# Spectral weights in rows of 4096 B: one transfer a tile for rows 256 to 511

## The chip, the cores and the metric

The kernel runs on one core of a Trainium2 chip. The time is device microseconds of one execution; of each kernel several executions are taken, and the median counts.

## What is computed

Forgetting attention over 8 batches and 8 heads (576 positions, 64 wide), then a spectral mix over the 512 joined channels, and a channel mix with a residual:

```python
attn = softmax(scale * q @ k.T + decay)          # causal, decay from cumsum(log f)
x = (attn @ v) joined over heads                 # [8, 576, 512]
X = np.fft.rfft(x, axis=1)                       # 64 modes are kept
Yr = einsum('bmd,mde->bme', Xr, w_r) - einsum('bmd,mde->bme', Xi, w_i)
Yi = einsum('bmd,mde->bme', Xr, w_i) + einsum('bmd,mde->bme', Xi, w_r)
u = x + np.fft.irfft(Y, n=576, axis=1)
out = u + np.maximum(u @ w_ch, 0.0)
```

`w_r` and `w_i` are [64, 512, 512] in f32, 67 MB each. The kernel works in bf16 with f32 sums; the transfers that GpSimd (POOL) issues convert on the way.

## The kernel before

**Attention.** 32 pairs (four groups `g` of two heads, 8 batches `b`, in the order of `g`). In each step `i` of a loop, POOL issues the loads of pair `i+3` (`load_qk` line 107, `load_v` line 119), VectorE (DVE) scales v (line 319), TensorE (PE) makes the scores (line 351) and the weighted sums (line 396), ScalarE (ACT) the exponentials (line 358), and q and k of the next pair are transposed (line 306; copied by DVE, line 311). Two steps later `dft` (line 423) turns the finished 128 channels of one group and batch into a spectrum: five matmuls over the 576 positions with a table of three blocks of 64 modes (-im, re, im), summed in one PSUM tile of 128 channels x 192. ACT copies it (line 430) into `XS[channel, g, ...]`, where one mode's 24 columns (three blocks x 8 batches) lie together.

**Weights.** Modes are taken in 16 units `u` of four, channels in four quarters `dc` of 128 rows of each matrix. A tile (u, dc) holds a quarter of four modes of both matrices, as bf16 [128, 2, 4, 512]: two transfers (`w_r`, `w_i`), each 4 x 128 rows of 2048 B at the source, 1024 B in SBUF. The list `wseq` has all (u, 0), then (0, 1) to (5, 1), then the rest by unit. Tiles have 7 buffers; in program order POOL is 6 tiles ahead of the matmuls. A transfer of POOL's queue also waits for the one eight transfers before it, whose completion semaphore it takes over.

**Spectral matmuls.** `spec_mms` (line 160) has eight matmuls for a tile, four modes in four strips of 32 PSUM partitions: the 32 (16 and the neighbours') spectrum columns as weights, 512 columns of `w8` moving. From step 10 on `spec_early` takes one tile of the list's first 22 in each attention step. The last unit runs the other way around: `spec_cols` (line 175) has the `w8` blocks as weights and 16 spectrum columns moving, 32 matmuls for a tile.

**After attention**, for each unit: the remaining quarters (2 and 3, from unit 6 on also 1); for eight of them `xw` (lines 535 and 549), which multiplies x with `w_ch`; from unit 12 on `fold` (lines 591 to 597), which adds the first 96 of 128 real and imaginary parts of the spectrum back for a batch; then the sums `Yb` (line 631) are turned by matmuls with `perm` (line 634). In the last unit, quarter 3 is split: 16 matmuls of `w_r`, an add, the first output block's bases (line 672), 16 matmuls of `w_i`, an add (line 730). Then 20 blocks of output (`rest`, line 687, ACT line 745, DVE line 746) leave on SyncE's queue.

The order is written out by hand (a manual schedule); nothing is moved by a planner.

Of the kernel before, what the change touches and what calls it, by code (L numbers as in the profile page):

```python
# [10 lines left out]
F32 = mybir.dt.float32  # L11
BF16 = mybir.dt.bfloat16
I32 = mybir.dt.int32
ALU = mybir.AluOpType
# [9 lines left out]
def kernel(  # L24
# [11 lines left out]
    nc = tc.nc  # L36
    B, H, S, Dh = q.shape
    NM = moe_w_r.shape[0]
    D = H * Dh
    assert S == 576 and Dh == 64 and D == 512 and H == 8, (B, H, S, Dh)  # L40
    assert NM == 64 and B == 8
    NSB = 5
    SBLK = [128, 128, 128, 128, 64]
    NEB = D // 128
    BH = B * H
    NPAIR = B * H // 2
    NU = NM // 4
# [5 lines left out]
    XROW = 24 * NM + 32  # L53
# [8 lines left out]
    const = ctx.enter_context(tc.tile_pool(name="const", bufs=1))  # L62
    wpool = ctx.enter_context(tc.tile_pool(name="wpool", bufs=NW))
    yxpool = ctx.enter_context(tc.tile_pool(name="yxpool", bufs=8))

    x_all = const.tile([128, B, NSB, D], BF16, name="x_all")
    XS = const.tile([128, NEB, XROW], BF16, name="XS")
    wch = const.tile([128, NEB, D], BF16, name="wch")
    ident_bf = const.tile([128, 128], BF16, name="ident_bf")
    ident_f = const.tile([128, 128], F32, name="ident_f")  # L70
# [4 lines left out]
    bas3 = const.tile([128, NSB, 3, NM], BF16, name="bas3")  # L75
# [5 lines left out]
    accT = const.tile([128, NEB, B, 8], F32, name="accT")  # L81
# [13 lines left out]
    psM = actx.enter_context(tc.tile_pool(name="psM", bufs=2, space=PSUM))  # L95
# [36 lines left out]


    early = [(u, 0) for u in range(NU)] + [(u, 1) for u in range(NX)]
    wseq = early + [(u, dc) for u in range(NU) for dc in range(1, NEB) if (u, dc) not in early]
    wtile = {}
    wissued = [0]

    def issue_w():
        if wissued[0] >= len(wseq):  # L140
            return
        u, dc = wseq[wissued[0]]
        wissued[0] += 1
        w8 = wpool.tile([128, 2, 4, D], BF16, tag="w8", name="w8")
        for t, src in enumerate((moe_w_r, moe_w_i)):
            step = 1 if t == 1 and wissued[0] == len(wseq) else 4
            for j in range(0, 4, step):
                m = 4 * u + j
                nc.gpsimd.dma_start(  # L149
                    w8[:, t, j : j + step, :],  # L150
                    src[m : m + step, dc * 128 : (dc + 1) * 128, :].rearrange("m p e -> p m e"),
                )
        wtile[(u, dc)] = w8

    def spec_mms(A, u, dc, first, last):
        w8 = wtile.pop((u, dc))
        for t in range(2):
            for j in range(4):
                c0 = (4 * u + j) * 24 + (8 if t == 0 else 0)
                nc.tensor.matmul(  # L160
                    A[32 * j : 32 * j + 32, :],
                    lhsT=XS[:, dc, c0 : c0 + 32],
                    rhs=w8[:, t, j, :],
                    start=(first and t == 0),
                    stop=(last and t == 1),
                )

    def spec_cols(AT, dc, ts):
        u = NU - 1
        w8 = wtile[(u, dc)]  # L170
        for j in range(4):
            for eb in range(NEB):
                for t in ts:
                    c0 = (4 * u + j) * 24 + (8 if t == 0 else 0)
                    nc.tensor.matmul(
                        AT[:, eb, 2 * j : 2 * j + 2, :].rearrange("p c b -> p (c b)"),
                        lhsT=w8[:, t, j, eb * 128 : (eb + 1) * 128],
                        rhs=XS[:, dc, c0 : c0 + 16],
                        start=(t == ts[0]),
                        stop=(t == ts[-1]),  # L180
                    )


# [13 lines left out]
    load_v(0)  # L197
    masks.make_identity(nc, ident_bf[:])
    issue_w()
    load_qk(1)  # L200
    load_v(1)
# [64 lines left out]
    def setup_late():  # L266
        nc.vector.memset(XS[:, :, 24 * NM : XROW], 0.0)
        nc.vector.tensor_copy(
# [148 lines left out]

    def dft(i):
        g, b = pairs[i]
        pd = psM.tile([128, 3, NM], F32, tag="m", name="pd")  # L420
        for sc in range(NSB):
            ns = SBLK[sc]
            nc.tensor.matmul(  # L423
                pd[:],
                lhsT=x_all[:ns, b, sc, g * 128 : g * 128 + 128],
                rhs=bas3[:ns, sc, :, :],
                start=(sc == 0),
                stop=(sc == NSB - 1),
            )
        nc.scalar.copy(  # L430
            XS[:, g, 0 : 24 * NM].rearrange("p (m c b) -> p c m b", c=3, b=8)[:, :, :, b], pd[:]
        )

    yacc = {}
# [1 line left out]
    def spec_early(u, dc):  # L436
        if u == NU - 1:
            AT = psM.tile([128, NEB, 8, B], F32, tag="m", name="AT0")
            spec_cols(AT, dc, (0, 1))
            nc.vector.tensor_copy(accT[:], AT[:].rearrange("p e c b -> p e b c"))  # L440
            return
        A = psM.tile([128, D], F32, tag="m", name="A0")
        spec_mms(A, u, dc, True, True)
        if dc == 0:
            if u % 2 == 0:
                yacc[u // 2] = yxpool.tile([128, 2, D], F32, tag="yx", name="yacc")
            nc.scalar.copy(yacc[u // 2][:, u % 2, :], A[:])
        else:
            y = yacc[u // 2][:, u % 2, :]
            nc.vector.tensor_tensor(y, A[:], y, ALU.add)  # L450
# [9 lines left out]
    for i in range(NPAIR + 2):  # L460
# [35 lines left out]
        if i >= 2:  # L496
            dft(i - 2)
# [8 lines left out]
        if i >= 10 and spec_done < len(early):  # L506
            spec_early(*early[spec_done])
            spec_done += 1
# [3 lines left out]
    with ExitStack() as bctx:  # L512
# [8 lines left out]
        with ExitStack() as mctx:  # L521
# [81 lines left out]
            for u in range(NU):  # L603
                last = u == NU - 1
                if not last:
                    A = psA.tile([128, D], F32, tag="a", name="A1")
                first = 2 if u < NX else 1
                for dc in range(first, NEB - 1 if last else NEB):
                    if dc == NEB - 1 and u in xw_plan:
                        xw(xw_plan[u])  # L610
                    split = NSB
                    if u >= NF and dc < 3:
                        b = 2 * (u - NF) + dc - 1
                        split = 2 if b == B - 1 else NSB
                        ys = fold_modes(b)
                        fold(b, ys, range(split))
                    if last:
                        AT = psA.tile([128, NEB, 8, B], F32, tag="a", name="AT1")
                        spec_cols(AT, dc, (0, 1))
                        nc.vector.tensor_tensor(  # L620
                            accT[:], AT[:].rearrange("p e c b -> p e b c"), accT[:], ALU.add
                        )
                    else:
                        spec_mms(A, u, dc, dc == first, dc == NEB - 1)
                    issue_w()
                    if split < NSB:
                        fold(b, ys, range(split, NSB))
                if last:
                    break
                Yb = ybpool.tile([128, D], BF16, tag="yb", name="Yb")  # L630
                nc.vector.tensor_tensor(Yb[:], A[:], yacc[u // 2][:, u % 2, :], ALU.add)  # L631
                yps = psT.tile([128, NEB, 64], F32, tag="t", name="yps")
                for eb in range(NEB):
                    nc.tensor.matmul(
                        yps[:, eb, :],
                        lhsT=Yb[:, eb * 128 : (eb + 1) * 128],
                        rhs=perm[:],
                        start=True,
                        stop=True,
                    )  # L640
                if u < NF:
                    ydst = YT[:, :, :, 8 * u : 8 * u + 8]
                else:
                    ydst = YL[:, :, :, 8 * (u - NF) : 8 * (u - NF) + 8]
                nc.vector.tensor_copy(
                    ydst,
                    yps[:].rearrange("p eb (b c) -> p eb b c", b=8),
                )

        usb = bctx.enter_context(tc.tile_pool(name="usb", bufs=4))  # L650
        psU = bctx.enter_context(tc.tile_pool(name="psU", bufs=4, space=PSUM))
# [43 lines left out]
        def last_modes(h):  # L695
# [22 lines left out]
            nc.scalar.copy(yl[h][0][:], py[:])  # L718
            nc.vector.tensor_copy(yl[h][1][:], pyw[:])

        AT = psU.tile([128, 2, NEB, 8, B], F32, tag="u", name="AT2")
        spec_cols(AT[:, 0, :, :, :], NEB - 1, (0,))
        nc.vector.tensor_tensor(
            accT[:], AT[:, 0, :, :, :].rearrange("p e c b -> p e b c"), accT[:], ALU.add
        )
        first = bases(0)
        spec_cols(AT[:, 1, :, :, :], NEB - 1, (1,))
        for h in range(2):
            bs = slice(4 * h, 4 * h + 4)
            nc.vector.tensor_tensor(  # L730
                YL[:, :, bs, KL - 8 : KL],
                AT[:, 1, :, :, bs].rearrange("p e c b -> p e b c"),
                accT[:, :, bs, :],
                ALU.add,
            )
# [51 lines left out]
```

## Time and profile before

| what | value |
|---|---|
| median of 3 runs | 457.81 us (457.38 to 460.25) |
| profiled execution | 458.9 us, its span 457.1 us |
| granted TensorE clock | 0.825 |
| busy PE, DVE, ACT, POOL | 75%, 54%, 48%, 42% |
| moved by DMA | 96.66 MB, mean 211 GB/s |
| read from HBM | 163.73 MB |
| first tile with the second half's pace | from 233 us |

A busy PE is not PE at its peak, and an engine's share over the whole span mixes two stages: attention with early tiles up to some 230 us, then the weight stage, then output from 424 us. "DMA share" is the time that packets took over that of 16 DMA engines; packets of one engine overlap, so it can be over 1. GB/s counts what is written, so a converting load reads twice as much.

### The profile page before, as it was taken

The numbers are of one execution on the slowest core, as the hardware profiler recorded it, in microseconds if no ns is written. First come the engines' busy times: TensorE is split into PE (matmuls) and PEld (weight loads), VectorE is DVE, ScalarE is ACT, GpSimd is POOL, SyncE is SP. The second block draws the span as 40 slices with busy tenths as digits, with TensorE's granted clock in tenths as the row PEclk, the third lists the DMA queues.
The fourth block names the chain that finished last, engine by engine and source line by source line (L and its number), as shares of the span: only waits on it lengthen the run. The fifth ranks groups of instructions, "written<-read, shape, count | busy, mean of one in ns | idle before, by whom it ended". The sixth has DMA issues, their size and how long they took to land.

```text
span 457.1 us, 8638 instructions
## 1 busy us (share of the span) xinstructions
PE 343.5 (75%) x3448; PEld 171.7 (38%) x3448; DVE 244.6 (54%) x632; ACT 220.2 (48%) x325; POOL 193.7 (42%) x280
## 2 busy tenths in 40 slices
PE   1587796997787877868988487678666499778993
PEld 1254464554444434543533133223232133234331
DVE  7597786985665747576832122212121066356785
ACT  5476475786656565645722121122022066354673
POOL 9574646957466666565332332233223222310000
PEclk9999677997968787766997767777577599899998
DMA  9999999999999999999999999999999999998598
GB/s 161 204 198 209 197 224 206 170 225 212 222 214 222 217 224 216 224 210 218 208 207 205 206 206 206 206 206 206 207 206 207 207 206 206 206 206 148 197 339 294
DMA packets 89432, 96.66 MB, mean 211 GB/s; under 512 B 8400, under 2 KB 82640, under 8 KB 89392
## 3 DMA queue, kind: packets, MB, share of 16 engines
q0 software_dynamic: 80608, 85.61, 108.7%
q1 hardware_dynamic: 8784, 10.50, 6.9%
q8 instruction: 27, 0.44, 0.4%
q14 instruction: 13, 0.11, 0.1%
HBM read 163.73 MB, written 9.44 MB: 379 GB/s over the span
## 4 chain that ended last, share of the span: by engine, by line
DMA 72%; PE 13%; POOL 6%; DVE 5%; issue 3%; DVEq 0%; POOLq 0%
DMA w<-in_moe_w_i_dram 56%; DMA vt<-in_v_dram 11%; POOL vt L119 3%; DMA qk<-in_k_dram 2%; DMA wch<-in_moe_w_ch_dram 2%; PE U L672 2%; PE Z L672 2%; POOL w L149 2%; DVE qkT L311 2%; PE pav L396 2%; POOL qk L107 1%; PE U L687 1%; PE sps L351 1%; PE pd L423 1%; DVE vs L319 1%
## 5 line engine op out<-in xcount | busy, mean ns | idle before, releaser
L358 ACT ACTIVATE et<-sps 128x1024 bf16<-128x1024 f32 x96 | 96.0, 1042 | 20.7 <-PE sps L351 20.5
L149 POOL DMA_DIRECT2D w<-in_moe_w_r_dram x64 | 48.2, 754 | 84.1 <-DMA w<-in_moe_w_r_dram 24.0
L149 POOL DMA_DIRECT2D w<-in_moe_w_i_dram x67 | 49.8, 744 | 68.6 <-DMA w<-in_moe_w_i_dram 63.1
L160 PE MATMUL A<-w,XS 128*32 128x512 bf16 x480 | 45.7, 448 | 34.5 <-DMA w<-in_moe_w_i_dram 23.4
L556 ACT CAST XW<-pxw 128x512 bf16<-128x512 f32 (+1 forms) x40 | 23.4, 585 | 96.9 <-PE pxw L549 89.5
L396 PE MATMUL pav<-vs,et 128*128 128x65 bf16 (+1 forms) x896 | 58.9, 211 | 0.0
L396 PEld LDWEIGHTS <-et 128*128 128x128 bf16 (+1 forms) x896 | 42.4, 111 | 29.6 <-issue 27.7
L119 POOL DMA_DIRECT2D vt<-in_v_dram x58 | 45.2, 785 | 18.5 <-DMA w<-in_moe_w_i_dram 5.8
L311 DVE COPY qkT<-tp 128x640 bf16<-128x640 bf16 x64 | 48.9, 764 | 6.1 <-PE tp L306 5.9
L351 PE MATMUL sps<-qkT 64*128 64x512 bf16 (+4 forms) x320 | 46.3, 357 | 4.3 <-ACT et L358 2.5
L430 ACT CAST XS<-pd 128x192 bf16<-128x192 f32 x32 | 33.2, 1045 | 32.7 <-PE pd L423 32.6
L631 DVE TENSOR_TENSOR Yb<-A,yacc 128x512 bf16<-128x512 f32 x15 | 10.4, 691 | 69.4 <-PE A L160 69.4
L319 DVE TENSOR_TENSOR vs<-vt,wT 128x512 bf16<-128x512 f32 x32 | 22.1, 689 | 47.4 <-DMA vt<-in_v_dram 47.3
L549 PE MATMUL pxw<-wch,xT 128*128 128x512 bf16 (+1 forms) x160 | 47.0, 457 | 0.0
L306 PE MATMUL tp<-ident_bf,qk 128*64 128x128 bf16 x576 | 32.6, 248 | 13.1 <-DMA qk<-in_k_dram 12.4
L411 DVE TENSOR_TENSOR x_all<-pav,rcp 128x384 bf16<-128x384 f32 (+2 forms) x96 | 36.2, 377 | 3.4
L598 DVE TENSOR_TENSOR XW<-pz,XW 128x512 bf16<-128x512 f32 (+1 forms) x40 | 27.0, 690 | 20.2 <-PE pz L597 19.9
L540 DVE COPY xT<-ptr 128x576 bf16<-128x576 bf16 x32 | 14.6, 457 | 37.8 <-PE ptr L535 37.6
L107 POOL DMA_DIRECT2D qk<-in_k_dram x32 | 19.8, 619 | 31.5 <-DMA w<-in_moe_w_i_dram 29.4
L160 PEld LDWEIGHTS <-XS 128*32 128x32 bf16 x480 | 9.8, 97 | 53.0 <-issue 47.5
L342 PE MATMUL s<-qkT 64*64 64x64 bf16 x64 | 7.3, 213 | 27.9 <-DVE qkT L311 27.9
L306 PEld LDWEIGHTS <-qk 128*64 128x64 bf16 x576 | 21.3, 123 | 18.5 <-DMA qk<-in_q_dram 12.0
(111 smaller groups left out, 510.6 us busy)
## 6 DMA issues: line engine op xcount, KB each, us to landing
w<-in_moe_w_r_dram POOLq DMA_DIRECT2D x64, 512.0 KB, 19.3
w<-in_moe_w_i_dram POOLq DMA_DIRECT2D x63, 512.0 KB, 20.0
out_dram<-o_sb SPq DMA_DIRECT2D x16, 512.0 KB, 3.5
vt<-in_v_dram POOLq DMA_DIRECT2D x58, 128.0 KB, 7.5
qk<-in_q_dram POOLq DMA_DIRECT2D x32, 144.0 KB, 9.4
qk<-in_k_dram POOLq DMA_DIRECT2D x32, 144.0 KB, 8.3
out_dram<-o_sb SPq DMA_DIRECT2D x8, 128.0 KB, 3.3
vl<-in_v_dram POOLq DMA_DIRECT2D x14, 64.0 KB, 7.5
```

Of the source, the lines that this page charges most:

```text
L119: q_v.dma_start(vt[:, 4 * hp : 4 * hp + 4, :], v[b, 2 * g + hp, 0:512, :].rearrange("(c p) d -> p c d", p=128),)
L149: nc.gpsimd.dma_start(w8[:, t, j : j + step, :], src[m : m + step, dc * 128 : (dc + 1) * 128, :].rearrange("m p e -> p m e"),)
L160: nc.tensor.matmul(A[32 * j : 32 * j + 32, :], lhsT=XS[:, dc, c0 : c0 + 32], rhs=w8[:, t, j, :], start=(first and t == 0), stop=(last and ...
L306: nc.tensor.transpose(tp[64 * hp : 64 * hp + 64, r - r0, :, :].rearrange("p n c -> p (n c)"), qk[:, hp, r * 64 : r * 64 + 64], ident_bf[:, :],
L311: nc.vector.tensor_copy(st[i]["T"][:].rearrange("p n (c r) -> p n c r", r=9)[:, :, :, r0:r1], tp[:, 0 : r1 - r0, :, :].rearrange("p r n c ...
L351: nc.tensor.matmul(ps[:, hp, c : c + n], lhsT=KT[sl, jb * 128 : jb * 128 + 128], rhs=QT[sl, i0 : i0 + n], start=True, stop=True,)
L358: nc.scalar.activation(st[i]["et"][:, T, :, :], ps[:], ACT.Exp, scale=scale)
L396: nc.tensor.matmul(pav[:Ms, sb % 3, hp, :], lhsT=eblk(i, hp, jb, sb), rhs=rhs, start=(jb == 0), stop=(jb == sb),)
L411: nc.vector.tensor_tensor(x_all[:ns, b, lo:hi, g * 128 : g * 128 + 128].rearrange("p s (h d) -> p s h d", h=2), pav[:ns, lo % 3 : lo % 3 + ...
L430: nc.scalar.copy(XS[:, g, 0 : 24 * NM].rearrange("p (m c b) -> p c m b", c=3, b=8)[:, :, :, b], pd[:])
L549: nc.tensor.matmul(pxw[:Ms, :], lhsT=xT[:, eb, sb * 128 : sb * 128 + Ms], rhs=wch[:, eb, :], start=(eb == 0), stop=(eb == NEB - 1),)
L598: nc.vector.tensor_tensor(XW[b][:Ms, sb, :], pz[:Ms, :], XW[b][:Ms, sb, :], ALU.add)
```

## The change

Quarters 0 and 1 stay. Rows 256 to 511 of a matrix (quarters 2 and 3) are now taken together: tile (u, 2) is these rows of `w_r` for four modes, tile (u, 3) the same of `w_i`. Partition p takes rows 256 + 2p and 257 + 2p, which lie side by side, 4096 B at the source and 2048 B in SBUF. A tile is one transfer, the last one four (one for each mode; before, the last tile had one transfer of `w_r` and four of `w_i`). The list has the same order of (u, dc).

The spectrum has to be split the same way: even and odd channels of the upper 256. For groups 2 and 3, `dft` runs twice, on channels with a step of two, into 64 PSUM partitions (0 to 63 for group 2, 64 to 127 for group 3), and ACT's copy goes to a new tile `XP[p, even/odd, 24 columns, mode]`, where one column's 64 modes lie together and the 24 columns of a mode are 128 B apart. `XS` keeps groups 0 and 1. In the last unit, quarter 3 is no longer split: its 32 matmuls come after the first bases.

```diff
-    XS = const.tile([128, NEB, XROW], BF16, name="XS")
+    XS = const.tile([128, 2, XROW], BF16, name="XS")
+    XP = const.tile([128, 2, 24, NM], BF16, name="XP")
...
         u, dc = wseq[wissued[0]]
         wissued[0] += 1
-        w8 = wpool.tile([128, 2, 4, D], BF16, tag="w8", name="w8")
-        for t, src in enumerate((moe_w_r, moe_w_i)):
-            step = 1 if t == 1 and wissued[0] == len(wseq) else 4
+        if dc < 2:
+            w8 = wpool.tile([128, 2, 4, D], BF16, tag="w8", name="w8")
+            for t, src in enumerate((moe_w_r, moe_w_i)):
+                nc.gpsimd.dma_start(
+                    w8[:, t, :, :],
+                    src[4 * u : 4 * u + 4, dc * 128 : (dc + 1) * 128, :].rearrange("m p e -> p m e"),
+                )
+        else:
+            w8 = wpool.tile([128, 4, 2, D], BF16, tag="w8", name="w8")
+            src = (moe_w_r, moe_w_i)[dc - 2]
+            step = 1 if wissued[0] == len(wseq) else 4
             for j in range(0, 4, step):
                 m = 4 * u + j
                 nc.gpsimd.dma_start(
-                    w8[:, t, j : j + step, :],
-                    src[m : m + step, dc * 128 : (dc + 1) * 128, :].rearrange("m p e -> p m e"),
+                    w8[:, j : j + step, :, :].rearrange("p m r e -> p m (r e)"),
+                    src[m : m + step, 256:512, :].rearrange("m (p r) e -> p m (r e)", r=2),
                 )
...
+    XPv = XP[:].rearrange("p r c m -> p (r c) m")
...
-        for t in range(2):
+        for n in range(2):
             for j in range(4):
-                c0 = (4 * u + j) * 24 + (8 if t == 0 else 0)
+                m = 4 * u + j
+                st_, sp_ = first and n == 0, last and n == 1
+                if dc < 2:
+                    M = 32
+                    c0 = m * 24 + (8 if n == 0 else 0)
+                    lhsT, rhs = XS[:, dc, c0 : c0 + 32], w8[:, n, j, :]
+                else:
+                    M = 32 if st_ else 16
+                    c0 = 24 * n + (8 if dc == 2 else 0)
+                    lhsT, rhs = XPv[:, c0 : c0 + M, m], w8[:, j, n, :]
                 nc.tensor.matmul(
...
+                    A[32 * j : 32 * j + M, :], lhsT=lhsT, rhs=rhs, start=st_, stop=sp_
+                )
...
+        pd = psM.tile([128, 2, 3, NM], F32, tag="m", name="pd2")
+        half = slice(64 * (g - 2), 64 * (g - 2) + 64)
+        for r in range(2):
+            for sc in range(NSB):
+                ns = SBLK[sc]
+                nc.tensor.matmul(
+                    pd[half, r, :, :],
+                    lhsT=x_all[:ns, b, sc, g * 128 + r : g * 128 + 128 : 2],
+                    rhs=bas3[:ns, sc, :, :],
+                    start=(sc == 0),
+                    stop=(sc == NSB - 1),
+                )
         nc.scalar.copy(
-            XS[:, g, 0 : 24 * NM].rearrange("p (m c b) -> p c m b", c=3, b=8)[:, :, :, b], pd[:]
+            XP[half, :, :, :].rearrange("p r (c b) m -> p r c b m", c=3)[:, :, :, b, :], pd[half]
         )
...
-        AT = psU.tile([128, 2, NEB, 8, B], F32, tag="u", name="AT2")
-        spec_cols(AT[:, 0, :, :, :], NEB - 1, (0,))
-        nc.vector.tensor_tensor(
-            accT[:], AT[:, 0, :, :, :].rearrange("p e c b -> p e b c"), accT[:], ALU.add
-        )
         first = bases(0)
-        spec_cols(AT[:, 1, :, :, :], NEB - 1, (1,))
+        AT = psU.tile([128, NEB, 8, B], F32, tag="u", name="AT2")
+        spec_cols(AT, NEB - 1)
```

`spec_cols` picks its operands for quarters 2 and 3 in the same way as `spec_mms` (16 columns of `XPv` moving, `w8[:, j, n, ...]` as weights).

## The prediction

> **What bounds the kernel now.** I read the page's row of DMA first: the engines are busy in every slice up to the last weights. The table of stretches shows what that means in the second half (columns: stretch, its length, busy time of PE, PE's weight loads, DVE, ACT, POOL with counts, granted clock, DMA share, GB/s).
>
> ```profile
> 120.00:160.00 40.00, 31.48 (x392) 17.80 (x390) 25.47 (x80) 24.36 (x32) 24.72 (x36) 0.74 1.22 218
> ...
> 274.00:314.00 40.00, 28.63 (x180) 12.38 (x181) 8.47 (x18) 5.85 (x10) 11.61 (x16) 0.71 1.24 206
> 314.00:355.00 41.00, 29.00 (x181) 11.73 (x180) 7.01 (x14) 8.77 (x15) 11.85 (x16) 0.75 1.24 206
> ...
> 420.00:424.00 4.00, 3.61 (x50) 1.83 (x48) 1.83 (x5) 1.17 (x2) 0.00 (x0) 1.00 0.10 18
> ```
>
> From 233 to 417 us the rate is 206 GB/s in every stretch, whatever the engines do. The chain of waits says the same as a period:
>
> ```profile
> 253.43 20.05 DMA w<-in_moe_w_i_dram
> 273.77 20.05 DMA w<-in_moe_w_i_dram
> 294.11 20.05 DMA w<-in_moe_w_i_dram
> ```
>
> Eight transfers of 512 KB, four tiles, take 20.34 us from one start to the next: 5.085 us a tile (4 x 1.0486 MB / 20.34 = 206 GB/s). A tile reads twice what it writes (f32 in, bf16 out): 412 GB/s at the source. It has 1024 rows of 2048 B, 64 for each of the 16 DMA engines, so one row takes 79.5 ns. Third, the list of waits: who waits for whom.
>
> ```profile
> DVE vs L319 <- DMA vt<-in_v_dram: 47.3, 19, 3.3
> ...
> PE A L160 <- DMA w<-in_moe_w_i_dram: 23.4, 12, 2.6
> ...
> PE tp L306 <- DMA qk<-in_k_dram: 12.4, 9, 4.0
> ...
> PE A L160 <- DMA w<-in_moe_w_r_dram: 10.4, 9, 1.9
> ```
>
> In both halves the engines wait for the stream, not the stream for them. Last, the end, where the stream meets TensorE (start, length):
>
> ```profile
> 417.28 0.93 PE L175 MATMUL AT<-XS,w 128*128 128x16 bf16 x31 [0.81 <-DMA w<-in_moe_w_i_dram]
> ...
> 420.34 0.56 PE L175 MATMUL AT<-XS,w 128*128 128x16 bf16 x16
> ...
> 420.76 0.59 PE L672 MATMUL U<-x_all,ident_bf 128*128 128x512 bf16 x2
> ...
> 421.26 0.61 PE L672 MATMUL Z<-XW,ident_bf 128*128 128x512 bf16 x2
> ...
> 421.70 0.66 PE L175 MATMUL AT<-XS,w 128*128 128x16 bf16 x16
> ```
>
> The last wait for weights ends at 417.28 (tile (15,2)); from there PE works without a gap into the output blocks. So the time is the stream up to tile (15,2), plus 40 us of PE work and output.
>
> **The change, part by part. The rows.** Sixteen units have two tiles each with the new rows, 32 in all; each becomes 512 rows of 4096 B, 32 for each DMA engine. The order of tiles, the bytes and the buffers (7) stay. What a 4096 B row costs no row of this trace shows; bytes alone make it 2 x 79.5 = 158.9 ns. A fixed part in each row can be read from the attention stage, where short rows are mixed in. At 219 GB/s (160 to 216 us) one pair with one tile (1.0486 + 0.2949 + 0.2949 MB written) takes 7.48 us. Less 5.085 for the tile, 2.40 us are left for q and k (16 rows of 2304 B for each engine) and v (72 rows of 256 B). With a row costing o + s x bytes, two equations hold: o + 2048 s = 79.5 and 88 o + 55296 s = 2400. They give s = 0.0368 ns/B and o = 4.2 ns. A 4096 B row is then 154.7 ns: 4.2 ns saved, 32 times a tile, 0.134 us, and 31 tiles up to (15,2) give 4.2 us. The mix is the weak place: with 222 GB/s (160 to 180 us) o is 2.5 ns and the saving 2.5 us, with 217 (180 to 216 us) 5.2 ns and 5.2 us; if q and k rows cost no more than 2048 B ones, o is 6.6 ns and it is 6.5 us. Zero holds if the source side is limited by bytes. A loss isn't excluded: if v paid for bytes alone (0.71 us), q and k would be left with 1.69 us, 105 ns a row, 18% more per byte than at 2048 B, and 32 tiles at that are +29 us. I take 4.2: the line by the mean rate, with both row lengths on it, in the middle of what the rates of that stage give.
>
> The Trainium skill (DMA: Bandwidth & Descriptors, "Why small descriptors are slow") puts about 3 cycles of overhead on each packet, with 32 B beats at 850 MHz: an estimate by it is 78.8 ns for 2048 B, near the measured 79.5, and 154.1 for 4096 B, which would save 3.5 us over 31 tiles. The same section holds joining descriptors worth it only up to 256 B, which speaks against the change; by that the saving is about 0. The same page ("iDMA fabric") gives a stream with 4 KiB rows 408.7 GB/s, less than the 412 here; by that the 32 tiles cost 1.5 us more. No run here shows 4096 B rows.
>
> **Fewer transfers.** 32 fewer on POOL's queue, about 0.75 us of issue each; they are hidden, since POOL waits for landings (63.1 and 29.5 us before line 149). Transfers wait for the one eight before them; with three tiles in four transfers, six tiles may be under way instead of four, and the buffers allow no fewer. The stream gets no emptier: 0.
>
> **Half a tile can no longer be used early.** PE took four of eight matmuls on the w_r half before the w_i half came; now it waits for the whole, and behind that wait stand Yb's turning matmuls (line 634) and the next unit. At (14,3) that makes 0.40 us after the landing into 0.61, 0.2 later; the wait of 0.81 at 417.28 covers it. Without that cover it is 0.2 at the end.
>
> **The spectrum.** For 16 pairs dft makes ten matmuls instead of five (same 192 columns), 0.69 to 1.09 us more PE work a pair. PE is idle 8.5 of 40 us from 120 to 160, 1.6 us in a pair's 7.5. Where nothing is awaited a pair takes 3.9 us (pd at 220.07 and 224.01), less than a tile's 5.085. So DMA waits hide it: 0; all of it on the path is 16 x 0.69 to 1.09, 11 to 17 us. ACT's copy goes from 1045 ns (192 elements written at a step) to something between 585 (line 556, 512 in a row) and 2090 (twice the elements); ACT is idle some 3 us a pair, so either is hidden.
>
> **Operands at a step of 128 B.** Weights of 16 or 32 columns now come from XP at a step, in the middle tiles under DMA waits of 2.6 to 6.5 us in each 20: 0. In (15,2) and the last tile the step is in the moving operand of 2 x 32 matmuls, now about 30 ns each. No such read is in the trace. The nearest row is ACT's stepped write, 1045/192 = 5.4 ns an element: 16 columns would take 87 ns, 64 x 57 = +3.6 us. A gain has no source there, the columns being the same. I take 0, since the write is another engine's, and keep 3.6 for the range.
>
> **The end.** Sixteen matmuls go from before the first bases to after them (DVE's add of their half falls away). U moves up, Z still waits until 421.26 (the last XW of line 598), then 32 matmuls (0.93) instead of 16 (0.56): +0.4. The last pieces are twice as large, with eight matmuls behind the last one instead of four; no bytes move from 422 on (0 GB/s), and PE would come to those eight at about 422.4 by the same clock, so they are in.
>
> **Sum:** -4.2 + 0.4 = -3.8 us, at the profiled execution's 458.9 us (span 457.1, 1.8 around it) 455.1. The median was 457.81, 1.1 lower, so 454.0.
>
> **Rivals.** *Bytes bind (14%).* The 206 GB/s don't move in any stretch, and the source side may be full: the row saves nothing, the end costs 0.4: 458.2. Against it: the pairs with short rows need more time than their bytes. *A larger fixed part (10%).* The 6.5 us above, less 0.4: 451.7. For it: v's 72 short rows are the larger part of the 2.40 us; against it: q and k rows would be free of their extra bytes. *Long rows slower (11%).* In the 32 tiles, from 233 us on, a 4096 B row costs more than two of 2048. It decides against the change by 1% from 163 ns a row (4.1 x 32 x 32 = 4.2 us, and 0.4); at half of the 18% it is +15, 473. For it: q and k rows longer than 2048 B can't be priced apart from v; against it: the 2.40 us are shared without it when short rows carry a fixed part, which the rates of that stage all give. *The spectrum on the path (7%).* 11 us, less 4.2 and with 0.4: 465. It needs PE's 1.6 us of idle per pair to be time that can't be used. *The change doing less than it says* is no case: the new transfers are one a tile with 1024 elements a row.
>
> **Numbers.** My forecast has 58%, between 452.4 (o of 5.9, half way from 5.2 to 6.6) and 457.6 (the stepped operand at its worst). What can be told from no change is about 1%, 4.6 us: faster means below 453.2, slower above 462.4. Some 18 of the 58 lie below 453.2 (an o above 5.0), with the larger fixed part 28%. Slower: 9 of 11 and 6 of 7, 15%. The rest is 57%. The range from 451 to 461 leaves out those 15 above, one or two of the slow cases between, and some 3 below.
>
> **What would show it.** In the profile after: a new tile in 4.95 us, so 212 GB/s instead of 206 while only new tiles come (the first twelve), then 210 (one old and two new); still DMA at 1.2 and waits of PE for w. The last wait for weights near 413.1, and from there 0.4 us more to the first output. A rate still at 206 shows bytes binding; below 206, slow rows. If DMA's share falls under 1 before 216, the spectrum is on the path. If AT's 32 matmuls take over 2 us at the end, the stepped operand is priced wrong.

## The result, and the profile after

| | median | range | executions |
|---|---|---|---|
| before | 457.81 us | 457.38 to 460.25 | 5 |
| after | 451.81 us | 450.49 to 453.41 | 5 |

The ratio is 0.9859, 95% interval 0.9822 to 0.9896: 6.0 us faster, where 3.8 were forecast. On another chip it was 0.989 (the last experiment), 5.3 us by the medians. The profiled execution after took 452.24 us, its span 450.5; before 458.9 and 457.1.

The table of stretches of the profile after (columns as in the prediction):

```profile
120.00:160.00 40.00, 30.85 (x415) 18.38 (x415) 25.30 (x79) 22.15 (x32) 23.80 (x35) 0.87 1.21 219
240.00:260.00 20.00, 11.70 (x101) 5.00 (x100) 5.18 (x10) 3.50 (x6) 4.52 (x7) 0.81 1.12 212
274.00:314.00 40.00, 30.76 (x185) 13.56 (x191) 7.72 (x16) 8.31 (x15) 7.41 (x10) 0.76 1.17 210
314.00:355.00 41.00, 24.62 (x166) 10.36 (x164) 7.01 (x14) 6.28 (x11) 8.14 (x11) 0.70 1.16 210
413.00:417.00 4.00, 3.08 (x45) 1.79 (x46) 1.50 (x4) 0.81 (x2) 0.00 (x0) 1.00 0.16 31
```

212 GB/s while only new tiles come, then 210 with one old tile for two new ones, where 206 stood; attention with early tiles (the first line) went from 218 to 219, and around the last matmuls of the weights (the last line) hardly anything moves, as before. The same in the chain of waits (start, length):

```profile
234.10 30.24 DMA w<-in_moe_w_i_dram
264.88 29.44 DMA w<-in_moe_w_i_dram
294.85 29.95 DMA w<-in_moe_w_i_dram
```

Eight transfers are now six tiles, four new (one transfer each) and two old (two each). From 264.88 to 294.85 they take 29.97 us. Less two old tiles at 5.085 that leaves 4.95 for a new one: 0.135 us saved a tile, 154.7 ns for a row of 4096 B. One step of the chain is a rough measure (the next, to 325.33, is 30.48 us). By the moments at which packets landed a new tile takes 4.98 us (220 to 257 us) and an old one, before, 5.10 (235 to 395): 0.12 saved.

The waits (total us, times, the longest one):

```profile
DVE vs L343 <- DMA vt<-in_v_dram: 46.7, 21, 3.6
...
PE A L182 <- DMA w<-in_moe_w_r_dram: 21.9, 7, 3.8
...
PE tp L330 <- DMA qk<-in_k_dram: 12.6, 12, 4.4
...
PE A L182 <- DMA w<-in_moe_w_i_dram: 10.4, 4, 3.9
```

The engines still wait for the stream, by nearly the same sums as before. One wait is gone, at the end:

```profile
399.78 0.65 PE L182 MATMUL A<-w,XP 128*16 128x512 bf16 x8 [1.94 <-DMA w<-in_moe_w_i_dram]
...
410.16 1.07 PE L199 MATMUL AT<-XP,w 128*128 128x16 bf16 x32
...
414.26 0.61 PE L713 MATMUL Z<-XW,ident_bf 128*128 128x512 bf16 x2 [0.53 <-DVE XW L639]
414.70 1.25 PE L199 MATMUL AT<-XP,w 128*128 128x16 bf16 x32
```

Before, TensorE waited 0.81 us for tile (15,2) until 417.28. Now it comes to that tile at 410.16 and finds it there; its last wait for weights is the one for (14,3), at 399.78.

Where the 6.6 us between the two spans went can be read from the packets: the moment at which so many MB had been written divides each execution at the same place of the work. Up to 42 MB the stream holds attention and early tiles, from 25 MB on the time of the late pairs (groups 2 and 3); from 48 to 87 MB it holds the tiles of the second half. In us, one profiled execution each, the experiments below included:

```
                                   0-25 MB  25-42  42-48  48-87  to the end
before                               123.6   77.7   28.3  189.1   38.4
before, early copies twice           123.3   78.1   27.9  189.1   38.4
before, late copies twice            123.7   78.0   28.0  189.1   38.8
change, XP laid out as XS     4096 B 122.1   78.0   27.3  185.6   38.1
change with 2048 B rows              123.1   77.1   27.9  189.2   38.2
before, new layout alone             123.2   75.7   28.0  189.0   37.9
after                         4096 B 123.5   76.1   27.3  185.5   38.1
after, another chip           4096 B 120.6   76.6   27.3  185.5   39.6
change, two transfers a tile  4096 B 120.7   75.9   27.4  186.0   40.3
change, last tile split       4096 B 123.8   76.5   27.2  185.5   37.9
new layout for all groups     4096 B 125.0   77.5   27.3  185.6   38.6
the same, last tile split     4096 B 123.6   77.0   27.3  185.6   38.3
the same, 16 early columns    4096 B 123.3   77.5   27.3  185.5   38.5
```

From before to after: 4.6 us in the stages with the new rows (1.0 and 3.6), 1.6 us in the stage of the late pairs, where no new row comes but in its last 1.4 us, and 0.3 at the end. The forecast had the first part only. Each row is one execution, and executions of one kernel differ by 2 us and more; a difference between two rows counts for little by itself, one between groups of rows for more.

### The profile page after: what moved, and what is told of

It is laid out like the page before. It is cut to its first block, busy times and chain, and to the rows that moved or that the text cites. A ratio compares the mean times of both kernels' runs of the same rounds, so it can differ in the third digit from the quotient of the medians.

```text
span 450.5 us, 8747 instructions
## 1 busy us (share of the span) xinstructions
PE 340.2 (76%) x3518; PEld 175.3 (39%) x3528; DVE 243.5 (54%) x631; ACT 212.0 (47%) x325; POOL 170.0 (38%) x248
## 2 busy tenths in 40 slices
DMA packets 72536, 96.66 MB, mean 215 GB/s; under 512 B 7888, under 2 KB 49360, under 8 KB 72496
## 4 chain that ended last, share of the span: by engine, by line
DMA 65%; PE 16%; POOL 8%; issue 5%; DVE 3%; ACT 1%; DVEq 0%; POOLq 0%; ACTq 0%
DMA w<-in_moe_w_i_dram 53%; DMA vt<-in_v_dram 8%; DMA w<-in_moe_w_r_dram 4%; POOL vt L120 4%; PE U L713 2%; POOL w L150 2%; PE Z L713 2%; POOL qk L108 2%; PE A L182 2%; PE U L728 1%; PE pd L464 1%; PE pz L638 1%; PE pav L420 1%; PE pu L632 1%; PE pu L635 1%
## 5 line engine op out<-in xcount | busy, mean ns | idle before, releaser
L420 PE MATMUL pav<-vs,et 128*128 128x65 bf16 (+1 forms) x896 | 57.4, 208 | 0.0
L420 PEld LDWEIGHTS <-et 128*128 128x128 bf16 (+1 forms) x896 | 41.2, 109 | 28.2 <-issue 26.3
L375 PE MATMUL sps<-qkT 64*128 64x512 bf16 (+4 forms) x320 | 44.8, 347 | 3.5 <-ACT et L382 2.0
L182 PE MATMUL A<-w,XP 128*16 128x512 bf16 (+1 forms) x240 | 22.5, 463 | 32.9 <-DMA w<-in_moe_w_r_dram 21.9
L590 PE MATMUL pxw<-wch,xT 128*128 128x512 bf16 (+1 forms) x152 | 42.8, 430 | 1.5 <-DVE xT L581 1.3
L150 POOL DMA_DIRECT2D w<-in_moe_w_r_dram x32 | 24.4, 764 | 41.3 <-PE A L182 32.9
L160 POOL DMA_DIRECT2D w<-in_moe_w_i_dram x19 | 13.3, 701 | 66.2 <-DMA w<-in_moe_w_i_dram 31.4
L150 POOL DMA_DIRECT2D w<-in_moe_w_i_dram x32 | 24.6, 769 | 12.2 <-DMA w<-in_moe_w_i_dram 11.9
L160 POOL DMA_DIRECT2D w<-in_moe_w_r_dram x16 | 11.9, 744 | 42.4 <-DMA w<-in_moe_w_r_dram 22.6
L636 ACT CAST x_all<-pu 128x512 bf16<-128x512 f32 (+1 forms) x40 | 23.4, 584 | 8.0 <-PE pu L635 7.0
```

Of the source, the lines that this page charges most:

```text
L150: nc.gpsimd.dma_start(w8[:, t, :, :], src[4 * u : 4 * u + 4, dc * 128 : (dc + 1) * 128, :].rearrange("m p e -> p m e"),)
L182: nc.tensor.matmul(A[32 * j : 32 * j + M, :], lhsT=lhsT, rhs=rhs, start=st_, stop=sp_)
L375: nc.tensor.matmul(ps[:, hp, c : c + n], lhsT=KT[sl, jb * 128 : jb * 128 + 128], rhs=QT[sl, i0 : i0 + n], start=True, stop=True,)
L420: nc.tensor.matmul(pav[:Ms, sb % 3, hp, :], lhsT=eblk(i, hp, jb, sb), rhs=rhs, start=(jb == 0), stop=(jb == sb),)
L590: nc.tensor.matmul(pxw[:Ms, :], lhsT=xT[:, eb, sb * 128 : sb * 128 + Ms], rhs=wch[:, eb, :], start=(eb == 0), stop=(eb == NEB - 1),)
```

## The experiments

The first four ran on one chip, the next four on a second, the last four on a third, each time beside the kernel before (457.84, 458.49 and 458.05 us).

**New spectrum, old rows.** All of the change but the rows: even and odd rows of a tile come in two transfers of 2048 B rows.

```diff
...
+            for n in range(2):
+                step = 1 if n == 1 and wissued[0] == len(wseq) else 4
+                for j in range(0, 4, step):
+                    m = 4 * u + j
+                    nc.gpsimd.dma_start(
+                        w8[:, j : j + step, n, :],
+                        src[m : m + step, 256:512, :].rearrange("m (p r) e -> p m r e", r=2)[:, :, n, :],
+                    )
...
```

> The split spectrum, the new tiles and the new end stay; each new tile comes in two transfers of 512 KB, one for the even and one for the odd rows, so its rows are 2048 B again (at a pitch of 4096 B). If the row's fixed cost is what the change saved in the weight stage (0.138 us a tile by the rate of 210 GB/s, 4.3 us), this loses all of it: 206 GB/s from 233 us on. If rows and transfers are all there is to the change, the time is 457.8 to 458.3 (the end costs up to 0.4). If the some 2 us that the change gained beyond the row's 4.3 less 0.4 come from the spectrum's shorter copy on ACT (473 instead of 1041 ns for 16 pairs), they stay here: 455.5 to 456.5, and a pair of the attention stage from 130 to 212 us still takes 7.4 us instead of 7.65.

Measured: 454.98 us, ratio 0.9939 (0.9914 to 0.9964), at 206 GB/s again. So nearly half of the gain does not come from the rows, though the ten matmuls and the new end are in this kernel.

**New rows, two transfers a tile.**

```diff
-            step = 1 if wissued[0] == len(wseq) else 4
+            step = 1 if wissued[0] == len(wseq) else 2
```

> Rows of 4096 B stay, but each new tile comes in two transfers of 512 KB (two modes each), so again only four tiles' worth of transfers may be under way. If row length is all that counts, nothing changes: 451.5 to 452.3, 210 to 212 GB/s from 233 us on. If the gain beyond the rows comes from fewer transfers (the queue is emptied less often in the attention stage, from 188 us on, where the first new tiles are issued), it goes: 453 to 454, and the rate from 180 to 216 us falls from 226 towards 217 GB/s.

Measured: 452.17 us, ratio 0.9875 (0.9833 to 0.9917), 209 to 211 GB/s: near the change's rate and, within the intervals, its time. The number of transfers makes no difference that this measurement shows. Against the kernel above, which also has two transfers a tile, the rows are worth 0.0064 of the time, 2.9 us.

**The last tile split around the first bases.**

```diff
+        AT = psU.tile([128, NEB, 8, B], F32, tag="u", name="AT2")
+        spec_cols(AT, NEB - 1, (0, 1))
         first = bases(0)
-        AT = psU.tile([128, NEB, 8, B], F32, tag="u", name="AT2")
-        spec_cols(AT, NEB - 1)
+        spec_cols(AT, NEB - 1, (2, 3))
```

> Only the end differs: of the last tile's 32 matmuls the 16 of the first two modes come before the first bases again. By the prediction's step on the end (0.4 us lost) this is 0.4 us faster, 451.4, and the add of YL starts about 0.4 to 0.6 us sooner after the last fold. If the stream's last bytes set the end instead (they move until 415), the matmuls wait for the weights before the bases and nothing is gained: 451.8 or more.

Measured: 451.1 us, ratio 0.9844 (0.9811 to 0.9877). It is the lowest median of all, 0.7 below the change, but the intervals overlap and its last column in the table is that of the change (37.9 and 38.1): not settled.

**The new spectrum in the old layout.** `XP` laid out as `XS` was (one mode's 24 columns side by side): TensorE reads in a row, ACT writes at a step, twice as many elements as before.

```diff
-    XP = const.tile([128, 2, 24, NM], BF16, name="XP")
+    XP = const.tile([128, 2, XROW], BF16, name="XP")
...
-                    M = 32 if st_ else 16
+                    M = 32
...
```

> Rows and transfers as in the change; only the layout of the split spectrum differs: the 24 columns of a mode lie together as in XS, so PE's operands have no step and ACT's copy is stepped again, with twice the elements of the copy before: about 2.0 us (1045 ns for 192 elements) instead of 473 ns, in 16 pairs. If ACT's short copy made the attention stage faster, that is lost here and more: 454 or above, 7.6 us or more a pair between 130 and 212 us. If it is hidden, as the prediction had it, the time is that of the change less up to 0.3 us for the 64 matmuls of the last unit without a step (0.96 instead of 1.07 and 1.25 us): 451.5 to 452.

Measured: 454.13 us, ratio 0.9919 (0.9892 to 0.9945), with the change's 210 to 212 GB/s. The copy took 1916 ns (median; 1937 in the mean below: busy us, mean ns, idle us before it) against 473 in the change:

```profile
L471 ACT CAST XP<-pd 64x384 bf16<-64x384 f32 x16 | 30.5, 1937 | 24.6 <-PE pd L464 24.6
```

The rows' gain is there, the other part isn't: 78.0 in the table's second column, as before. By the medians it is 2.3 us above the change. From these four I took the length of ACT's copy to be the rest of the gain.

**The new layout alone.** The kernel before, but groups 2 and 3 go to a tile `XQ` in the new layout (five matmuls, old rows, old end); the matmuls of quarters 2 and 3 read it at a step of 128 B, the second four of a tile with 16 columns as in the change.

```diff
...
+            nc.scalar.copy(
+                XQ[:, g - 2, 0:24, :].rearrange("p (c b) m -> p c b m", c=3)[:, :, b, :], pd[:]
+            )
```

> The kernel before, with its rows, transfers, order and end; only the spectrum of groups 2 and 3 is kept with the 64 modes of a column together, so that ACT's copy (192 elements) writes in a row: about 0.33 us instead of 1.04 in 16 pairs, and PE reads its 16 or 32 columns at a step of 128 B. If the copy's length is what the change gained beyond the rows, this gains about as much as the kernel with 2048 B rows and the split spectrum did (2.9 us): 454.5 to 455.5. If it is the splitting of the spectrum or the other tile order that gained, this stays at 457.3 to 458.3. In both cases 206 GB/s from 233 us on.

Measured: 455.55 us, ratio 0.9939 (0.9916 to 0.9961), the same as the first experiment. ACT's copy took 319 ns:

```profile
L443 ACT CAST XQ<-pd 128x192 bf16<-128x192 f32 x16 | 5.1, 319 | 17.0 <-PE pd L431 16.9
```

The layout alone gives 2.9 us, and most of the gain lies in the late pairs (75.7 against 77.7). Since this kernel has five matmuls for a spectrum and the first experiment ten, and the ratios are the same, the doubled matmuls show no cost in the time; in the late pairs' column the first experiment is 1.4 us above this one (one execution each).

**The new layout for all groups, and the same with the last tile split.** If a short copy helps in 16 pairs, it should in 32.

```diff
-    XS = const.tile([128, 2, XROW], BF16, name="XS")
+    XS = const.tile([128, 2, 40, NM], BF16, name="XS")
...
+                XS[:, g, 0:24, :].rearrange("p (c b) m -> p c b m", c=3)[:, :, b, :], pd[:]
```

> The change, with the layout of the upper half used for groups 0 and 1 too: ACT's copy is short in all 32 pairs (about 0.33 instead of 1.04 us in the first 16). If ACT's copy lies on the path where the pairs don't wait for weights (pairs of 5.1 us between 80 and 101 us, ACT busy 17 of 20 us), the first 16 pairs gain up to 16 x 0.7 = 11 us of ACT's time, of which the stream can use what it isn't full of; from the upper half's 2.3 us a like amount would be 449.5 to 450.5. If ACT's copy is hidden, 451.5 to 452.

> The same with half of the last tile's matmuls before the first bases: by the split end alone, 0.4 to 0.7 us less than without it. If both add up, 449 to 450, the fastest of all; if neither counts, 451 to 452.

Measured: 454.35 us, ratio 0.992 (0.9893 to 0.9946), and with the split 453.75, 0.991 (0.9877 to 0.9943): no gain over the change. By the ratios the first is 1.4 to 2.8 us slower than the change in its two measurements, though its interval overlaps both of theirs. The early copies shrank to 319 ns, and TensorE's early weights now come at a step:

```profile
L182 PE MATMUL A<-w,XS 128*32 128x512 bf16 x240 | 24.7, 495 | 0.0
L182 PEld LDWEIGHTS <-XS 128*32 128x32 bf16 x240 | 8.0, 186 | 4.1 <-issue 2.6
L455 ACT CAST XS<-pd 128x192 bf16<-128x192 f32 x16 | 5.1, 319 | 17.6 <-PE pd L448 17.6
```

Against the change the weight loads grew from 97 to 186 ns and the matmuls of the early tiles from 447 to 495. Whether that is what takes the gain away isn't shown by this run.

**Row lengths by themselves.** A kernel that only moves weights, in sections of different rows; it leaves out attention and both mixes and writes zeros.

> Transfers alone, with nothing that waits for them; the output is written with zeros, and nothing of attention or of the mixes is computed. In turn: 12 tiles (2 MiB read, 1 MiB written each) with rows of 2048 B in two transfers, 12 with 4096 B in one, 12 with 4096 B in two, 12 with 8192 B, 12 with 1024 rows of 1024 B in four transfers (half a tile's bytes), 4 more with 2048 B. If a row costs 4.2 ns and 0.0368 ns/B on an engine: 206, 212, 212 and 215 GB/s written, and 41.9 ns a row of 1024 B, 195 GB/s. If bytes bind and the gain came from elsewhere, 206 GB/s in all. If the number of transfers counts, one and two transfers of 4096 B rows differ.

Measured, in stretches that lie within one section (length, DVE, POOL, clock, DMA share, GB/s): 2048 B, 4096 B in one transfer a tile, 4096 B in two, 8192 B, 1024 B. The first stretch starts at 70 us, since the output's zeros move beside the loads until 56.

```profile
70.00:90.00 20.00, 0.00 (x0) 5.58 (x9) 1.00 1.24 206
115.00:150.00 35.00, 0.00 (x0) 4.91 (x7) 1.00 1.12 212
160.00:195.00 35.00, 0.00 (x0) 9.82 (x14) 1.00 1.12 211
213.00:255.00 42.00, 0.00 (x0) 5.62 (x8) 1.00 1.06 214
275.00:305.00 30.00, 0.00 (x0) 25.44 (x37) 1.00 1.32 157
```

The stretch of 1024 B fell far below the line (195 expected), but it has four transfers for half a tile's bytes, and POOL was busy 25 of 30 us; so row length isn't the only thing that it measures.

**The copy made twice, late and early.** The kernel before with ACT's copy repeated, for groups 2 and 3, then for 0 and 1; nothing else differs.

```diff
-        nc.scalar.copy(
-            XS[:, g, 0 : 24 * NM].rearrange("p (m c b) -> p c m b", c=3, b=8)[:, :, :, b], pd[:]
-        )
+        for _ in range(2 if g >= 2 else 1):
+            nc.scalar.copy(
+                XS[:, g, 0 : 24 * NM].rearrange("p (m c b) -> p c m b", c=3, b=8)[:, :, :, b], pd[:]
+            )
```

> The kernel before, with ACT's copy of the spectrum made twice for the 16 pairs of groups 2 and 3 and nothing else changed: 16 x 1.04 us = 16.6 us more on ACT's queue, the operands of PE as they were. If the length of this copy is partly on the path, as the 2.9 us that the shorter copy gave suggest (2.9 of 16 x 0.72 = 11.6 us, a quarter), the time is some 4 us over before (ratio 1.009). If the 2.9 us came from something else in the new layout, it is within 1 us of before (ratio 0.998 to 1.002).

> The same doubling for the 16 pairs of groups 0 and 1 instead. If those copies are as much on the path as the later ones, again some 4 us over before (ratio 1.009), and the kernel with every copy short lost its gain elsewhere, to its stepped weights. If the early copies are hidden, within 1 us of before: then a short copy there had nothing to give.

Measured: 458.86 us, ratio 1.0013 (0.998 to 1.0046), and 457.69, 0.9989 (0.9963 to 1.0015). The page shows the added work (the first line is the kernel before), and no one pays for it:

```profile
L430 ACT CAST XS<-pd 128x192 bf16<-128x192 f32 x32 | 33.2, 1045 | 32.7 <-PE pd L423 32.6
L431 ACT CAST XS<-pd 128x192 bf16<-128x192 f32 x48 | 49.7, 1047 | 33.1 <-PE pd L423 32.6
```

16.5 us more on ACT, 0.8 us by the medians, and 78.0 in the table's second column, where the early doubling, which leaves the late pairs alone, has 78.1. The 4 us that the copy's length should have cost are outside the interval, which ends at 0.46%, 2.1 us: a copy as long again costs nothing that can be told from zero. So the length alone, more time for more nanoseconds, does not explain the gain; something else that the layout brings is likely.

**Sixteen stepped columns in the early tiles.** The kernel with the new layout for all groups, its second four matmuls of an early tile with 16 columns for 32.

```diff
-                    M = 32
+                    M = 32 if st_ else 16
```

> The kernel with every copy short (ratio 0.992), but the second four matmuls of an early tile load 16 stepped columns instead of 32: weight loads near 137 ns instead of 184 in half of the loads. If the stepped weights of the early tiles are what made that kernel slower than the change, the ratio falls from 0.992 to about 0.989 (half of the excess goes). If it is something else, it stays at 0.992.

Measured: 454.2 us, ratio 0.9927 (0.99 to 0.9954), no change. But the loads were not shortened as intended, to 137 ns in half of them:

```profile
L182 PEld LDWEIGHTS <-XS 128*32 128x32 bf16 x120 | 5.3, 165 | 4.0 <-issue 2.4
L182 PEld LDWEIGHTS <-XS 128*16 128x16 bf16 x120 | 5.3, 163 | 0.0
```

Both forms take about 164 ns (186 before), so it does not decide whether the stepped loads are what costs there.

**The change again.**

> The change itself beside the three others on one chip: ratio 0.986 within 0.002, the reference for them, whatever the theory.

Measured: 452.7 us, ratio 0.989 (0.9863 to 0.9917), 5.3 us. Its profile has the same 185.5 for the second half, and a stream that at 87 MB is 2.4 us ahead of that of the first profile; the end takes 1.6 us of that back (39.6 against 38.1). In the kernel with two transfers a tile it is the same (40.3). A likely reading is that TensorE, with xw, fold and the turning matmuls of the last units, sets the end where the stream comes earlier; no run tested it.

## Point by point

**What bounds the kernel** held for the second half, up to its end. The step "the time is the stream up to tile (15,2), plus 40 us of PE work" is the state of before; in the change TensorE's own chain from (14,3) on sets the end, 50.7 us against 50.9 from the last matmuls on (14,3) (399.78 and 406.17) to the end, and the last wait for weights is there, not near 413.1.

For the attention half the step "in both halves the engines wait for the stream, not the stream for them" failed. From 134 to 210 us, with the same old rows in all three, the kernel before with the early copies twice, with the late copies twice, and with the new layout alone:

```profile
134.00:210.00 76.00, 60.78 (x774) 34.62 (x771) 48.13 (x145) 45.53 (x57) 46.19 (x67) 0.73 1.21 217
134.00:210.00 76.00, 58.69 (x764) 34.19 (x760) 47.75 (x144) 54.93 (x69) 46.03 (x66) 0.75 1.21 218
134.00:210.00 76.00, 55.00 (x777) 32.41 (x776) 49.21 (x148) 39.19 (x58) 47.92 (x68) 0.84 1.21 222
```

The layout of a small tensor moved the rate from 217 to 222 GB/s at the same DMA share, so here the stream was not at its limit, though engines waited for transfers.

**The rows: right, in size too.** Forecast: 0.134 us a tile, 154.7 ns a row, 212 and then 210 GB/s. Measured: 0.12 to 0.135 us, 154.7 to 155.6 ns, 212 and 210. The table gives 4.6 us for the stages with new rows against 4.2 forecast for 31 tiles (4.3 if the stage from 42 to 48 MB is taken from all five rows of the table with 2048 B, 28.0 in the mean). The chip with both row lengths gives 2.9 by the ratios; there the kernel with new rows also has the longest end of the table (40.3), so part of what the stream gains seems to be lost where it meets TensorE. The kernel of transfers alone lies on the same line at 8192 B: 4.2 + 0.0368 x 8192 = 305.7 ns a row, 16 rows of each DMA engine in 4.89 us, 214 GB/s; it moved 214.

The way to the number was weaker than the number. It took the rate in attention for the stream's own pace, and it counted v's rows of 256 B one by one. Neither holds. In the stretch where 222 GB/s stood, the change ran at 226, with the same short rows and old tiles (its first new row comes at 198 us):

```profile
160.00:180.00 20.00, 16.80 (x203) 9.09 (x203) 11.08 (x36) 11.62 (x17) 13.05 (x19) 0.76 1.21 226
```

With 226 in the same two equations (1.6384 MB in 7.25 us, 2.17 for the short rows) o is 0.3 ns and the saving 0.3 us. And the page of before lists

```profile
DMA packets 89432, 96.66 MB, mean 211 GB/s; under 512 B 8400, under 2 KB 82640, under 8 KB 89392
```

where 72 rows of 256 B for each of 16 engines in 32 pairs would alone be 36 864 packets under 512 B. Most of v moved in packets of 4096 B (2080 of them in the trace), so the 88 rows of the equation were not 88 packets, and the equations did not price one. That the mean rate gave the right o was luck; two lengths of weight rows alone would have been the clean pair.

The Trainium skill (DMA: Bandwidth & Descriptors, "Why small descriptors are slow") has about 3 cycles a packet, an estimate of 154.1 ns for a 4096 B row; 154.7 to 155.6 was measured. The same section's remark that joining descriptors pays only up to 256 B is on putting several descriptors into one packet. The change made the rows longer instead (72536 packets in the whole execution, 89432 before), so the prediction's reading of it, a saving of about 0, did not apply: one row of 4096 B for two of 2048 B took 2.7% off the time of a tile (5.085 to 4.95 us).

**Fewer transfers: 0** held (two a tile or one: the rate within 1 GB/s, and no difference in time clear of the noise). **Half a tile can't be used early: 0** could not be seen apart: the 0.81 us that were to cover it are gone. In the first profile after no wait for weights follows (14,3), so a later start of that tile is no longer covered. After the last landing for (14,3) its matmuls took 0.65 us, 0.40 before; that is near the forecast's 0.2 and below what the medians resolve.

**The spectrum: half right, and here the sum went wrong.** Ten matmuls for five cost nothing, as forecast. The step that failed is "ACT's copy ... either is hidden", with the layout's effect on the late pairs put at 0. The copy became shorter than the lower bound of 585 ns:

```profile
L471 ACT CAST XP<-pd 64x384 bf16<-64x384 f32 x16 | 7.6, 473 | 24.7 <-PE pd L464 24.7
```

What the runs show in its place: the layout alone gives 2.9 us by the medians. By the profiles the late pairs' stage takes 76.3 us in the mean of the six with the late copy in a row and the early one stepped (75.7 to 77.1), and 77.9 in the four with both stepped (77.7 to 78.1): 1.6 us. The three with the new layout for all groups (77.0 to 77.5) lie between. The new rows in the old layout are 3.7 us below before, the new layout with the old rows 2.9, together 6.6, about the 6.0 of the change.

Why the layout helps stays open. ACT's time for the copy, and how long the copy holds its PSUM tile, are unlikely: the doubled copy has more of both. In the late pairs' stage TensorE doesn't yet read quarters 2 and 3 (in the change the first weight load from `XP` is at 228.8 us), so the stepped reads and the 16 columns can't act there. The granted clock rose with the layout, from 0.73 and 0.75 to 0.84 in the three lines above; but the new spectrum in the old layout had 0.82 in that stretch and 78.0 us in the stage, so the clock alone isn't it. That leaves the write itself, in a row or at a step, or an order of events that differs with the copy's end. No run compared a stepped copy with one in a row of the same length, so neither is shown.

**Operands at a step: 0** was near. The matmuls with a stepped moving operand took 190 ns for 170 before, a group of 32 took 1.07 and 1.25 us for 0.96, under the 2 us named as the sign of a wrong price: 0.4 us in both groups together, now on the path. One reading was too broad: the waits "of 2.6 to 6.5 us in each 20" are 1.1 in the stretch from 233 to 253 us. ACT's write was no measure for it: 1041 ns for 192 stepped elements against 319 in a row there, 12% here.

**The end: +0.4** can't be told apart. The end took no longer (38.1 against 38.4), and splitting the last tile gave 0.7 and 0.6 us less in two pairs of kernels, with overlapping intervals each time.

**The sum.** -4.2 + 0.4 against -6.0: the term for the rows was right, the layout's was missing. 451.81 us lies in the range of 451 to 461, but below the 452.4 to 457.6 that the forecast's 58% stood for, and below 453.2, where "faster" with its 28% began; on the other chip the ratio of 0.989 makes it 452.8. Of the rivals, bytes binding and slow rows are excluded by 212 GB/s, the spectrum on the path by the first and fifth experiments. The time of the larger fixed part, 451.7, was met, but by another mechanism: o is 4.2, not 6.6.

## What to carry to other kernels

A fixed cost per row can be read from one stream if two row lengths each run alone at their limit; a stage in which other work is mixed in gives a rate, not a limit, even where the DMA engines look full. When one edit also changes the layout of a small tensor, run that layout alone: here it was nearly half of the gain, though every engine that touched it had idle time. And before a gain is put down to a shorter instruction, lengthen that instruction: the doubled copy cost nothing that could be told from zero and took away a theory that three runs had agreed with.

## What the runs showed of the hardware

- A converting load from f32 to bf16 runs at 206, 212 and 214 GB/s written for rows of 2048, 4096 and 8192 B; the three lie on a line of 4.2 ns a row and 0.0368 ns a byte for a DMA engine.
- The f32 loads of v, 256 B a row and not converted, moved mostly in packets of 4096 B: 64 transfers of 128 KB and two of 64 KB make the 2080 that the trace of before has, the other 14 of 64 KB its 3584 packets of 256 B.
- ACT's copy of 192 elements a partition takes 319 ns when 64 lie in a row and 1041 when each is 48 B from the next; with 384 it is 473 and 1916. The Trainium skill (SBUF — State Buffer, "Door 1: The DMA port swizzle") says that an access that goes to a new 16-byte line pays a penalty; these numbers agree: 5.0 to 5.4 ns for each stepped element, 1.2 to 1.7 in a row.
- TensorE pays less: loading 16 weight columns that are 128 B apart took 128 to 134 ns in the mean in the second half and 163 in the early tiles, 32 of them 164 to 186, against 97 for 32 in a row; 16 moving columns at that step 190 against 170.
- The granted clock over the whole execution rose from 0.82 before (median) to between 0.83 and 0.85 in the kernels with the new spectrum, whose weights for `dft` are 64 columns instead of 128, but also to 0.83 in the new layout alone, which kept the 128. Over 65 executions of the kernel before, those with a higher clock were somewhat shorter (correlation -0.38, 0.8 us for 0.01). The new spectrum in the old layout had the change's clock (0.849 and 0.848, medians) and was 2.3 us slower; what part the clock has in the gain was not tried beyond that.
